# One stage's VectorE and ScalarE order left to the scheduler, its weight loads moved to the GpSimd queue, and the last output piece copied by one engine

## The chip, the cores and the metric

The kernel runs on one core of a Trainium2 chip. The metric is the device time in microseconds. Five engines take instructions, each in the order of its own queue: TensorE (PE in the profile) multiplies, VectorE (DVE) and ScalarE (ACT) work on tiles, GpSimd (POOL) and SyncE (SP) here only issue transfers (DMAs). SBUF holds the tiles, PSUM the sums of products.

## The reference

```python
# attention with decay: B, H, S, D = 4, 8, 768, 64
for t in range(S):
    state = gamma * state + outer(k[:, :, t], v[:, :, t])
    y[:, :, t] = scale * q[:, :, t] @ state
x = y.transpose(0, 2, 1, 3).reshape(3072, 512)
# first layer: w_in 512 x 2048, w_out 2048 x 512
h = x @ w_in
x = (h / (1 + exp(-1.702 * h))) @ w_out
# second layer, weights of the same sizes
h = x @ w_in2
P = a0 + a1*h + a2*h*h + a3*h*h*h
Q = 1 + abs(b0)*abs(h) + abs(b1)*h*h
out = (P / (Q + 1e-6)) @ w_out2
```

The inputs are 64-bit numbers as far as the weights go: a weight unit is read as pairs of 32-bit words.

## The kernel before

The 3072 tokens go in six blocks of 512. The first layer has 16 steps to a block, 96 in all, numbered through. In step j TensorE makes 12 products into a PSUM bank `hp` (`g1`, L1122). ScalarE takes the sigmoid z of it (`act1_a`, L1229), VectorE multiplies z by hp (L1230), and with that the bank is free. ScalarE rounds z to a high part gh (`act1_b`, L1238), VectorE takes the low part gl (L1239). Two steps later TensorE adds 12 products of gh and gl into four banks `o` (`g2`, L1143 to L1145). There are two banks for hp, which the attention's pY takes turns in too. So hp of step j+2, or pY and hp, can begin only when z of an earlier step has left its bank.

Three other things run beside the steps:

- The attention of the later blocks: one unit of 128 tokens (`att_unit`, L954) at four of a block's 16 steps. Its inputs are loaded (L735), scaled and turned by VectorE (`att_turn`), stored (L823) and fetched (L831), all by SP.
- The conversion of the second layer's weights, `conv2`: 32 units, four to a group g. A unit is loaded raw (`raw2`, L629 and L631) into one of four slots of 512 KB (pool `ws`, tag `s`). ScalarE begins (`w_first`, L561, "first" in this text), VectorE does four operations (L567, L569, L572, L583), ScalarE casts the high part (L619), VectorE takes the low part (L620). GpSimd stores it (`put`, L653 and L655). Between units 1 and 2 of a group come four sums (L682). `conv0` says at which step a group starts; a group takes the places x = -1 to 9, one a step.
- At a block's end the four banks `o` are copied (`evac`, L1153 and L1155) into tiles that take slots of the same pool `ws`, and stored by SP (L1156).

`step(i)` writes all this in a fixed order, the conversion at the end of the step. Steps 14 to 77 stand under `tc.manual_schedule(engines={E.PE, E.DVE, E.Activation, E.SP})`: on these four engines the order of the code is kept. On GpSimd, and in the steps from 78 on, a scheduler sets the order at build time: among the instructions that it takes to be ready, it picks the one that stands first in the code. `behind` keeps the raw loads in the code's order. The second layer follows in an order that its own planner writes. Its last output block is copied and stored in four pieces (`evac` inside `layer2`, L271 to L274).

Of the kernel before, what the change touches and what calls it, by code (L numbers as in the profile page):

```python
# [18 lines left out]
P = 128  # L19
# [4 lines left out]
KD = DM // P  # L24
# [37 lines left out]
def layer2(tc, pools, ab, XT, x_tile, XC, WC, WOT, load_wo, held, psum, out):  # L62
    nc = tc.nc
# [3 lines left out]
    NG = KF // 2  # L67
# [34 lines left out]
    for s in range(NSB):  # L102
        for g in range(NG):
            prev = [(s, g - 1, P4)] if g else []
            p = [(s, g, x) for x in (P1, P5, P6, P2, P3, P7)]
# [31 lines left out]
    def start_of(eng, deps):  # L137
        if any(d not in end for d in deps):
            return None
        return max([free[eng]] + [end[d] + (0.35 if d[0] in "PO" else 0.2) for d in deps])  # L140
# [4 lines left out]
    def h_any(half, n, name, dtype=F32):  # L145
        home, tag = SLOT[half, n]
        return home.tile([P, 2, 512], dtype, tag=tag, name=name)
# [114 lines left out]
    def evac(s, half, d):  # L262
        rows = s * 1024 + half * 512 + d * P
        last = (s, half) == (NSB - 1, 1)
        if last:
            t = h_any(0, d, f"os{s}_{half}_{d}")
            cut = 2 if d == 3 else 1
            for y in range(cut):
                m = slice(y * DM // cut, (y + 1) * DM // cut)
                if y or d % 2 and cut == 1:  # L270
                    nc.vector.tensor_copy(out=t[:, 0, m], in_=ACC[d][:, m])  # L271
                else:
                    nc.scalar.copy(out=t[:, 0, m], in_=ACC[d][:, m])
                nc.sync.dma_start(out=out[rows : rows + P, m], in_=t[:, 0, m])  # L274
            return
        if d % 2 == 0:
            EV[0] = h_any(half, 6 * half + d // 2, f"os{s}_{half}_{d}")
        t = EV[0]
        nc.scalar.copy(out=t[:, d % 2], in_=ACC[d])
        if d % 2:  # L280
            nc.sync.dma_start(out=out[rows - P : rows + P, :].rearrange("(x p) m -> p x m", p=P), in_=t)
# [103 lines left out]
    E = mybir.EngineType  # L385
    with tc.manual_schedule(engines={E.PE, E.DVE, E.Activation}):
# [7 lines left out]
        while pe < len(PEQ) or ready["DVE"] or ready["ACT"]:  # L394
            best = None
            if pe < len(PEQ):
# [4 lines left out]
                t = start_of("PE", deps)  # L401
                if t is not None:
                    best = (t, 0, "PE", None)
            for eng in ("DVE", "ACT"):
                c = [(start_of(eng, x[3]), x[2], n) for n, x in enumerate(ready[eng])]
                c = [x for x in c if x[0] is not None]
                if c:
                    t0 = min(x[0] for x in c)
                    _, rank, n = min((x for x in c if x[0] <= t0 + 0.05), key=lambda x: (x[1], x[2]))
# [3 lines left out]
            t, _, eng, n = best  # L413
            name = ("PE",)
            if eng == "PE":
                free["PE"] = t + 1.36
                if it[0] == "P":
                    s, g, p = PROD[it[1]]
# [10 lines left out]
            if name[0] in ("c4", "d3", "d7"):  # L429
                s, g = name[1:]  # L430
# [22 lines left out]
            while waiting and None in slots:  # L453
                m = min(waiting)
# [17 lines left out]
def tile_kernel(ctx: ExitStack, tc: tile.TileContext, q, k, v, w1i, w1o, w2i, w2o, pa, pb, cst, out):  # L472
    nc = tc.nc
# [47 lines left out]
    def unit(layer, u):  # L521
        return (ORD if layer == 1 else ORD2)[u]
# [86 lines left out]
    NG = KF // 2  # L609
# [3 lines left out]
    def behind(dma):  # L613

        tc.keep_in_program_order(dma)
# [6 lines left out]
    def raw2(u):  # L622

        nm, f = unit(2, u)
        src = {"i": w2i, "o": w2o}[nm].bitcast(I32)
        s = ws.tile([P, DM, 2], I32, tag="s", name=f"s2_{u}")
        if nm == "i":
            src = src[:, f * 2 * P : (f + 1) * 2 * P].rearrange("(c p) f -> p c f", p=P)
            behind(nc.sync.dma_start(out=s.rearrange("p (c f) t -> p c (f t)", c=KD), in_=src))  # L629
        else:  # L630
            behind(nc.sync.dma_start(out=s.rearrange("p f t -> p (f t)"), in_=src[f * P : (f + 1) * P, :]))  # L631
        STG[u] = RW[u] = s

    def word2(u):
        w_first(u)
        w_bits(u)
        w_sign(u, False)
# [4 lines left out]
    def parts(key, src, home):  # L642

        n = src.shape[1] // (2 * P)
        t = home.bitcast(F32R).rearrange("p a b -> p (a b)").rearrange("p (x h c) -> p x h c", x=n, h=2)
        split((t[:, :, 0], t[:, :, 1]), src.rearrange("p (x c) -> p x c", c=2 * P))
        OUT2[key] = t

    def put(key):
        t = OUT2.pop(key)  # L650
        g, x = key
        if x == "o":
            nc.gpsimd.dma_start(out=WO[g], in_=t.bitcast(F32))  # L653
        else:
            nc.gpsimd.dma_start(out=WC[g][x].rearrange("x p h k f -> p x (h k f)"), in_=t.rearrange("p x h c -> p x (h c)").bitcast(F32))  # L655

    def whole(f, src, home):
        t = home.bitcast(F32R).rearrange("p a b -> p (a b)").rearrange("p (h c) -> p h c", h=2)
        split((t[:, 0], t[:, 1]), src)
        OUT2[f, "o"] = t  # L660

    def conv2(g, x):

        u = 4 * g
        if x == -1:
            raw2(u)
        elif x == 0:
            raw2(u + 1)
            word2(u)
        elif x == 1:  # L670
            parts((g, 0), STG[u], RW.pop(u))
        elif x == 2:
            put((g, 0))
            word2(u + 1)
        elif x == 3:
            raw2(u + 2)
            a, b = STG.pop(u), STG.pop(u + 1)
            a11, a12, a21, a22 = a[:, : 2 * P], a[:, 2 * P :], b[:, : 2 * P], b[:, 2 * P :]
            t = SUM[g] = ws.tile([P, 4, 2 * P], F32, tag="s", name=f"sum{g}")
            A22S[g] = a22  # L680
            for y, p, q, op in ((0, a21, a22, ALU.add), (1, t[:, 0], a11, ALU.subtract), (2, a11, a21, ALU.subtract), (3, a12, t[:, 1], ALU.subtract)):
                nc.vector.tensor_tensor(out=t[:, y], in0=p, in1=q, op=op)  # L682
            parts((g, 1), t[:, 0:2].rearrange("p x c -> p (x c)"), RW.pop(u + 1))
        elif x == 4:
            put((g, 1))
        elif x == 5:
            raw2(u + 3)
            word2(u + 2)
            t = SUM.pop(g)
            parts((g, 2), t[:, 2:4].rearrange("p x c -> p (x c)"), RW.pop(u + 2))  # L690
            parts((g, 3), A22S.pop(g), t[:, 0:2])
        elif x == 6:
            put((g, 2))
            put((g, 3))
        elif x == 7:
            word2(u + 3)
            e = ws.tile([P, DM, 2], I32, tag="s", name=f"wo{2 * g}s")
            whole(2 * g, STG.pop(u + 2), e)
        elif x == 8:
            put((2 * g, "o"))  # L700
            whole(2 * g + 1, STG.pop(u + 3), RW.pop(u + 3))
        elif x == 9:
            put((2 * g + 1, "o"))
# [520 lines left out]
    def act1_a(j):  # L1224
        n = steps[j][4]
        hp = HP.pop(j)
        z = ch.tile([P, n], F32, tag="z", name=f"z{j}")
        CH[j] = z
        nc.scalar.activation(out=z, in_=hp, func=ACTF.Sigmoid, scale=1.702)  # L1229
        nc.vector.tensor_tensor(out=z, in0=hp, in1=z, op=ALU.mult)  # L1230
# [54 lines left out]
    for u in range(NU):  # L1285
        t = stage_tag(u)
# [9 lines left out]
    E = mybir.EngineType  # L1296
    with tc.manual_schedule(engines={E.SP}):
# [207 lines left out]
        conv0 = [KF + 2 + 9 * g - (0, 0, 0, 0, 1, 2, 3, 4)[g] for g in range(NG)]  # L1505
# [13 lines left out]
        def x_piece(i):  # L1519
            left = 2  # L1520
            while xq and left and (xq[0][0] or i > XS0 + 8):
# [10 lines left out]
                else:  # L1532
                    left -= 1
                    for f in xr[s, kk][n]:
                        if f:
                            f()

        def step(i):
            nonlocal nxt, j
            while nxt < NS and nxt - lead[steps[nxt][0]] <= i:  # L1540
                j = nxt
                nxt += 1
                g1(j)
                act1_a(j)
            if 0 <= i - KF + 2 < WHOLE:
                w_high(1, LATER[i - KF + 2], False)
                w_low(1, LATER[i - KF + 2], False)
            if i == KF:
                tc.keep_in_program_order(nc.scalar.activation(out=ab[:, 6:7], in_=ab[:, 5:6], func=ACTF.Abs))
            late = [f() for f in todo[i][0]]  # L1550
            if j >= FIRST_STEPS + 2 and j in CH:
                act1_b(j)
            for f in late:
                if f:
                    f()
            g2(i)
            layer, bi, fc, t0, n = steps[i]
            if fc == KF - 1 and bi < 5:
                evac(bi)
            late = [f() for f in todo[i][1]]  # L1560

            if i >= XS0:
                x_piece(i)
            if i >= NS - 4:
                load_wo(2 * (i - NS + 4))
                load_wo(2 * (i - NS + 4) + 1)
            if i == XS0 + 4:
                for kk in range(2):
                    t = xp.tile([P, 2, 512], F32, tag=f"xh{kk}_0", name=f"xb{kk}")
                    XB.append(t)  # L1570
                    for c in range(2):
                        nc.sync.dma_start(out=t[:, c], in_=x2[4][2 * c + kk])
            for g in range(NG):
                x = i - conv0[g]
                if x == 9:
                    conv2(g, x)
            for g in range(NG):
                x = i - conv0[g]
                if -1 <= x < 9:
                    conv2(g, x)  # L1580
            for f in late:
                if f:
                    f()

        with tc.manual_schedule(engines={E.PE, E.DVE, E.Activation, E.SP}):
            for i in range(FIRST_STEPS, XS0):
                step(i)
        for i in range(XS0, NS):
            step(i)
# [32 lines left out]
```

## Time and profile before

| | us |
|---|---|
| median of 3 runs (lowest, highest) | 1193.75 (1192.49, 1194.94) |
| the profiled execution | 1192.8 |
| its span | 1191.0 |
| TensorE busy in the span | 1119.5 (94%) |
| VectorE busy | 868.8 (73%) |
| ScalarE busy | 655.2 (55%) |
| GpSimd busy | 31.1 (3%) |

The profile is of one execution. Its time is 1.8 us above its span, which starts with the first instruction and ends with the last transfer. A row of the timeline is: start, duration, engine, line, operation, output and inputs, and in brackets the time that the engine had idled just before, with what ended that idle time. "SPq" and "POOLq" are the queues' DMA issues. Lines are those of the kernel before; in the kernel after, lines behind L684 are higher by 1 or 2.

### The profile page before, as it was taken

To read this page: it belongs to the slowest core of one execution; us is meant where nothing else is said; L and a number is where in the kernel's file an instruction comes from. 1 tells how busy PE (TensorE), PEld (TensorE's weight loads), DVE (VectorE), ACT (ScalarE), POOL (GpSimd) and SP (SyncE) were. 2 spreads that over 40 slices of the span, in tenths; PEclk is the share of its full clock that TensorE was granted. 3 is DMA by queue.
4 is the path that set the end of the run, shared out by engine and by line. 5 is a ranking of instruction groups with operands and counts; after the bars stand their busy time and mean duration, and the time that the engine had idled before them with its cause. 6 is when DMAs were issued, how large, how long until landed. Compare 5 with 4: busy or idle time off the path is not lost.

```text
span 1191.0 us, 18828 instructions
## 1 busy us (share of the span) xinstructions
PE 1119.5 (94%) x7217; PEld 911.8 (77%) x7217; DVE 868.8 (73%) x1192; ACT 655.2 (55%) x987; POOL 31.1 (3%) x52
## 2 busy tenths in 40 slices
PE   8999999698996879797999999999999999999998
PEld 6688878577775757586888888888888888888887
DVE  6999646375564445455577679999889899789895
ACT  5998322132232322222354569978778786787782
POOL 0000000000000000000000000000000000000000
PEclk9999999889998989899999999999999999999999
DMA  9944557565564554565278798583345561354100
GB/s 238 326 129 115 113 127 164 151 159 153 139 157 133 141 147 120 156 168 160 95 261 297 230 325 286 195 297 153 91 129 153 184 247 46 122 157 122 43 36 36
DMA packets 230394, 193.54 MB, mean 163 GB/s; under 512 B 153888, under 2 KB 178976, under 8 KB 230304
## 3 DMA queue, kind: packets, MB, share of 16 engines
q1 hardware_dynamic: 223904, 169.27, 49.4%
q0 software_dynamic: 6400, 23.07, 5.3%
q8 instruction: 57, 0.93, 0.3%
q14 instruction: 33, 0.27, 0.1%
HBM read 134.48 MB, written 57.67 MB: 161 GB/s over the span
## 4 chain that ended last, share of the span: by engine, by line
PE 66%; SPq 11%; DMA 9%; DVE 5%; issue 3%; ACT 2%; DVEq 0%; ACTq 0%
PE o L256 22%; PE hp L1122 13%; PE a L157 11%; SPq L735 7%; PE c L157 5%; DMA s<-in_moe_w_out_dram 4%; PE o L1143 3%; PE o L1144 3%; PE o L1145 3%; PE b L157 3%; DMA s<-in_moe_w_in_dram 2%; DMA xs<-x 2%; SPq L831 2%; SPq L823 1%; PE pY L954 1%
## 5 line engine op out<-in xcount | busy, mean ns | idle before, releaser
L1122 PE MATMUL hp<-xh,wi 128*128 128x512 f32 x768 | 266.7, 410 | 44.5 <-DVE z L1230 42.8
L1122 PEld LDWEIGHTS hp<-xh,wi 128*128 128x128 f32 x768 | 150.8, 196 | 81.8 <-DVE z L1230 45.9
L1122 PE MATMUL hp<-xl,wi 128*128 128x512 f32 x384 | 154.8, 404 | 0.0
L157 PE MATMUL a<-x,wi 128*128 128x512 f32 x576 | 145.3, 390 | 0.0
L1143 PE MATMUL o<-gh,wo 128*128 128x512 f32 x368 | 144.5, 393 | 0.0
L1144 PE MATMUL o<-gl,wo 128*128 128x512 f32 x368 | 143.6, 390 | 0.0
L1145 PE MATMUL o<-gh,wo 128*128 128x512 f32 x368 | 143.4, 390 | 0.0
L567 DVE TENSOR_SCALAR u<-u 128x512 f32<-128x512 f32 x64 | 27.0, 422 | 139.7 <-ACT u L561 139.7
L561 ACT ACTIVATE u<-s 128x512 f32<-128x512 f32 x64 | 43.1, 675 | 151.7 <-DMA s<-in_moe_w_in_dram 86.7
L157 PEld LDWEIGHTS a<-x,wi 128*128 128x128 f32 x576 | 108.0, 188 | 22.9 <-ACT b L180 0.4
L1238 ACT CAST gh<-z 128x512 fp32r<-128x512 f32 x80 | 49.6, 620 | 99.6 <-DVE z L1230 99.6
L1229 ACT ACTIVATE z<-hp 128x512 f32<-128x512 f32 x80 | 47.6, 595 | 86.3 <-PE hp L1122 80.1
L1230 DVE TENSOR_TENSOR z<-hp,z 128x512 f32<-128x512 f32 x80 | 54.9, 686 | 44.8 <-ACT z L1229 36.7
L1122 PEld LDWEIGHTS hp<-xl,wi 128*128 128x128 f32 x384 | 75.9, 198 | 15.2 <-issue 0.3
L320 DVE SCALAR_TENSOR_TENSOR z<-z,ab,w 128x1024 f32<-128x1024 f32 x48 | 61.6, 1283 | 28.4 <-ACT w L318 28.4
L1143 PEld LDWEIGHTS o<-gh,wo 128*128 128x128 f32 x368 | 69.7, 189 | 15.1 <-DVE wo L605 0.4
L1239 DVE TENSOR_TENSOR gl<-z,gh 128x512 fp32r<-128x512 f32 x80 | 54.7, 684 | 36.1 <-ACT gh L1238 35.0
L1144 PEld LDWEIGHTS o<-gl,wo 128*128 128x128 f32 x368 | 69.4, 189 | 14.6 <-DVE gl L1239 0.2
L1145 PEld LDWEIGHTS o<-gh,wo 128*128 128x128 f32 x368 | 69.2, 188 | 14.5
L157 PE MATMUL c<-x,wi 128*128 128x512 f32 x288 | 73.1, 389 | 0.0
L334 ACT ACTIVATE gh<-h 128x1024 fp32r<-128x1024 f32 x48 | 50.9, 1060 | 34.1 <-PE o L256 33.5
L338 DVE SCALAR_TENSOR_TENSOR gl<-h,gh 128x1024 fp32r<-128x1024 f32 x48 | 58.8, 1224 | 5.4 <-ACT gh L334 5.4
(246 smaller groups left out, 2203.5 us busy)
## 6 DMA issues: line engine op xcount, KB each, us to landing
wi<-wc SPq DMA_DIRECT2D x168, 256.0 KB, 2.9
s<-in_moe_w_in_dram SPq DMA_DIRECT2D x32, 512.0 KB, 5.6
s<-in_moe_w_out_dram SPq DMA_DIRECT2D x32, 512.0 KB, 5.2
x<-xc SPq DMA_DIRECT2D x28, 512.0 KB, 8.5
wc<-s POOLq DMA_DIRECT2D x24, 512.0 KB, 3.9
xc<-xo SPq DMA_DIRECT2D x36, 256.0 KB, 2.7
x<-os SPq DMA_DIRECT2D x20, 256.0 KB, 2.5
xs<-x SPq DMA_DIRECT2D x20, 256.0 KB, 4.3
```

Source lines behind the costliest of these rows:

```text
L157: nc.tensor.matmul(bank, wt[:, a, k], XT[s, x, k][:, b], start=begin and y == 0, stop=y == 5, skip_group_check=True)
L256: nc.tensor.matmul(ACC[d], a[:, x, r], w[:, b], start=g == 0 and x == 0 and y == 0, stop=g == NG - 1 and x == 1 and y == 2)
L320: dve("q", [("ab", m)], lambda: stt(out=v["z"], in0=v["z"], scalar=ab[:, 6:7], in1=v["w"], op0=ALU.mult, op1=ALU.add))
L334: nc.scalar.activation(out=GT[m][0], in_=h, func=ACTF.Copy, scale=-1.0)
L338: nc.vector.scalar_tensor_tensor(out=gl, in0=h, scalar=-1.0, in1=gh.bitcast(F32), op0=ALU.mult, op1=ALU.subtract)
L735: nc.sync.dma_start(out=t[HALF[n], NP * x : NP * x + NP, :], in_=heads[x])
L1122: nc.tensor.matmul(hp, w[:, kk, :], t[kk // 2][:, kk % 2, :], start=(x == 0), stop=(x == len(terms) - 1))
L1143: nc.tensor.matmul(o, wl[:, r], gh, start=a, stop=False)
L1144: nc.tensor.matmul(o, wh[:, r], gl, start=False, stop=False)
L1145: nc.tensor.matmul(o, wh[:, r], gh, start=False, stop=z)
L1230: nc.vector.tensor_tensor(out=z, in0=hp, in1=z, op=ALU.mult)
L1239: nc.vector.tensor_tensor(out=gl, in0=z, in1=gh.bitcast(F32), op=ALU.subtract)
```

## The change

The raw loads go from SP's queue to GpSimd's. Their place in the code stays at the end of the step (`conv2_load`), while the rest of `conv2` is called one step later, ahead of the step's own second half (`convert`). VectorE and ScalarE are taken out of the engines whose order is kept in steps 14 to 77. In the last output piece the second half is copied by ScalarE instead of VectorE and stored from ScalarE's queue.

```diff
-                if y or d % 2 and cut == 1:
+                if d % 2 and cut == 1:
                     nc.vector.tensor_copy(out=t[:, 0, m], in_=ACC[d][:, m])
                 else:
                     nc.scalar.copy(out=t[:, 0, m], in_=ACC[d][:, m])
-                nc.sync.dma_start(out=out[rows : rows + P, m], in_=t[:, 0, m])
+                (nc.scalar if y else nc.sync).dma_start(out=out[rows : rows + P, m], in_=t[:, 0, m])
...
-            behind(nc.sync.dma_start(out=s.rearrange("p (c f) t -> p c (f t)", c=KD), in_=src))
+            behind(nc.gpsimd.dma_start(out=s.rearrange("p (c f) t -> p c (f t)", c=KD), in_=src))
...
-            behind(nc.sync.dma_start(out=s.rearrange("p f t -> p (f t)"), in_=src[f * P : (f + 1) * P, :]))
+            behind(nc.gpsimd.dma_start(out=s.rearrange("p f t -> p (f t)"), in_=src[f * P : (f + 1) * P, :]))
...
+    def conv2_load(g, x):
+        n = {-1: 0, 0: 1, 3: 2, 5: 3}.get(x)
+        if n is not None:
+            raw2(4 * g + n)
...
+        def convert(i):
+            for g in sorted(range(NG), key=lambda g: i - conv0[g] != 9):
+                if 0 <= i - conv0[g] <= 9:
+                    conv2(g, i - conv0[g])
...
                 g1(j)
                 act1_a(j)
+            convert(i - 1)
...
             for g in range(NG):
-                x = i - conv0[g]
-                if x == 9:
-                    conv2(g, x)
-            for g in range(NG):
-                x = i - conv0[g]
-                if -1 <= x < 9:
-                    conv2(g, x)
+                conv2_load(g, i - conv0[g])
...
-        with tc.manual_schedule(engines={E.PE, E.DVE, E.Activation, E.SP}):
+        with tc.manual_schedule(engines={E.PE, E.SP}):
```

The order on TensorE is the same in both kernels, and SP's is the same without the raw loads. In the rows below z54 is z of step 54, u15 and s2_15 belong to weight unit 15, sum3 to group 3, and the last number of a name only tells tiles apart.

ScalarE from the sigmoid of step 54, before:

```order
L1229 ACTIVATE z54_4397<-hp54_4384 128x512
L1238 CAST gh54_4416<-z54_4397 128x512
L561 ACTIVATE u15_4520<-s2_15_4338 128x512
L619 CAST wo6s_4526<-u14_4340 128x512
L960 CAST xh4_0_4172<-pY_17_4432 128x2x128
L960 CAST xh4_1_4173<-pY_17_4432 128x2x128
L1229 ACTIVATE z55_4554<-hp55_4541 128x512
```

and in the change:

```order
L1230 ACTIVATE z54_4395<-hp54_4382 128x512
L1239 CAST gh54_4416<-z54_4395 128x512
L619 CAST s2_18_4786<-sum4_4814 128x2x256
L561 ACTIVATE u19_5080<-s2_19_4870 128x512
L619 CAST wo8s_5086<-u18_4888 128x512
L561 ACTIVATE u20_5126<-s2_20_5052 128x512
L619 CAST s2_19_4870<-u19_5080 128x512
L961 CAST xh4_0_4172<-pY_17_4432 128x2x128
L961 CAST xh4_1_4173<-pY_17_4432 128x2x128
L1230 ACTIVATE z55_4545<-hp55_4532 128x512
```

Between the same two sigmoids ScalarE now begins two units, 19 and 20, where it began unit 15.

VectorE from z of step 52 to z of step 53, before:

```order
L1230 TENSOR_TENSOR z52_4319<-hp52_4306,z52_4319 128x512
L1239 TENSOR_TENSOR gl52_4323<-z52_4319,gh52_4322 128x512
L567 TENSOR_SCALAR u14_4340<-u14_4340 128x512
L569 TENSOR_SCALAR s2_14_4256<-s2_14_4256 128x512
L572 SCALAR_TENSOR_TENSOR u14_4340<-u14_4340,s2_14_4256 128x512
L583 SCALAR_TENSOR_TENSOR u14_4340<-s2_14_4256,u14_4340 128x512
L620 TENSOR_TENSOR s2_14_4256<-sum3_4258,s2_14_4256 128x2x256
L620 TENSOR_TENSOR sum3_4258<-u13_4114,sum3_4258 128x256
L1230 TENSOR_TENSOR z53_4363<-hp53_4350,z53_4363 128x512
```

and in the change, from z of step 51 to z of step 52:

```order
L1231 TENSOR_TENSOR z51_4279<-hp51_4266,z51_4279 128x512
L567 TENSOR_SCALAR u15_4548<-u15_4548 128x512
L620 TENSOR_TENSOR wo6s_4554<-u14_4356,wo6s_4554 128x512
L1240 TENSOR_TENSOR gl51_4290<-z51_4279,gh51_4289 128x512
L572 SCALAR_TENSOR_TENSOR u15_4548<-u15_4548,s2_15_4338 128x512
L567 TENSOR_SCALAR u16_4594<-u16_4594 128x512
L583 SCALAR_TENSOR_TENSOR u15_4548<-s2_15_4338,u15_4548 128x512
L569 TENSOR_SCALAR s2_16_4520<-s2_16_4520 128x512
L572 SCALAR_TENSOR_TENSOR u16_4594<-u16_4594,s2_16_4520 128x512
L620 TENSOR_TENSOR s2_15_4338<-u15_4548,s2_15_4338 128x512
L583 SCALAR_TENSOR_TENSOR u16_4594<-s2_16_4520,u16_4594 128x512
L1231 TENSOR_TENSOR z52_4318<-hp52_4305,z52_4318 128x512
```

The work of two units is now mixed between z and gl of one step, and unit 16 comes at step 51; before it comes at step 55.

GpSimd's queue around the units 14 to 18, before:

```order
L655 DMA wc3_2_117<-s2_14_4256 128x2x512
L655 DMA wc3_3_118<-sum3_4258 128x512
L653 DMA wo6_141<-wo6s_4526 128x1024
L653 DMA wo7_142<-s2_15_4338 128x1024
L655 DMA wc4_0_119<-s2_16_4529 128x2x512
```

and in the change:

```order
L631 DMA s2_15_4338<-in_moe2_w_out_dram 128x1024
L655 DMA wc3_3_118<-sum3_4282 128x512
L629 DMA s2_16_4520<-in_moe2_w_in_dram 128x4x256
L655 DMA wc3_2_117<-s2_14_4256 128x2x512
L653 DMA wo6_141<-wo6s_4554 128x1024
L629 DMA s2_17_4573<-in_moe2_w_in_dram 128x4x256
L653 DMA wo7_142<-s2_15_4338 128x1024
L655 DMA wc4_0_119<-s2_16_4520 128x2x512
L631 DMA s2_18_4786<-in_moe2_w_out_dram 128x1024
```

The loads of units 15 to 18 now stand among the stores; unit 16's load stands ahead of unit 14's store, unit 18's behind that of unit 16.

## Rows read from the trace of the kernel before

**Rows 1.** Table by stretches: length, then busy time (instructions) by engine, clock, DMA.

```profile
core 0: us, PE busy (x) PEld busy (x) DVE busy (x) ACT busy (x) POOL busy (x), PEclk, DMA share, GB/s
...
149.46:606.75 457.29, 393.99 (x3369) 323.54 (x3368) 245.48 (x447) 124.88 (x234) 27.06 (x42) 0.93 0.56 147
606.75:697.19 90.44, 90.17 (x397) 74.09 (x396) 63.85 (x107) 43.47 (x75) 3.86 (x6) 1.00 0.81 284
```

**Rows 2.** Timeline, ScalarE's sigmoids of steps 74, 75 and 76.

```profile
569.59 0.60 ACT L1229 ACTIVATE z<-hp 128x512 f32<-128x512 f32 x1 [0.88 <-PE hp L1122]
577.31 0.60 ACT L1229 ACTIVATE z<-hp 128x512 f32<-128x512 f32 x1 [2.30 <-PE hp L1122]
582.75 0.60 ACT L1229 ACTIVATE z<-hp 128x512 f32<-128x512 f32 x1 [3.46 <-PE hp L1122]
```

**Rows 3.** TensorE's waits, 149.46 to 606.75 us: total, times, longest.

```profile
PE hp L1122 <- DVE z L1230: 42.5, 9, 9.6
PE pY L954 <- DVE z L1230: 17.2, 6, 4.1
PE pK L954 <- DMA rawv<-in_v_dram: 3.1, 1, 3.1
```

**Rows 4.** Chain of waits (start, length), and the table by stretches, around 240 us.

```profile
240.95 4.69 PE hp L1122 x12
...
248.38 2.72 PE hp L1122 x12
```

```profile
240.00:245.00 5.00, 4.05 (x10) 3.22 (x11) 4.93 (x10) 1.68 (x4) 0.00 (x0) 0.54 0.22 52
```

**Rows 5.** Timeline of ScalarE, 418 to 442 us.

```profile
423.13 0.62 ACT L619 CAST s<-u 128x512 fp32r<-128x512 f32 x1
437.04 0.66 ACT L561 ACTIVATE u<-s 128x512 f32<-128x512 f32 x1 [13.30 <-DMA s<-in_moe_w_in_dram]
437.61 0.58 ACT L1229 ACTIVATE z<-hp 128x512 f32<-128x512 f32 x1
```

**Rows 6.** Timeline of TensorE, 440 us.

```profile
440.60 0.79 PE L1122 MATMUL hp<-xh,wi 128*128 128x512 f32 x1 [8.15 <-DVE z L1230]
```

**Rows 7.** Timeline of SP's issues, 418 to 434 us.

```profile
421.55 5.29 SPq L735 DMA_DIRECT2D rawq<-in_q_dram  x4
...
432.27 1.09 SPq L629 DMA_DIRECT2D s<-in_moe_w_in_dram  x2
```

**Rows 8.** ScalarE's waits, 149.46 to 606.75 us.

```profile
ACT u L561 <- DMA s<-in_moe_w_in_dram: 86.7, 7, 15.5
...
ACT u L561 <- DMA s<-in_moe_w_out_dram: 56.5, 8, 10.4
```

**Rows 9.** DMA issues: queue, count, KB each, median us to landing.

```profile
wc<-s POOLq DMA_DIRECT2D x21, 512.0 KB, 3.9
s<-in_moe_w_in_dram SPq DMA_DIRECT2D x16, 512.0 KB, 4.9
...
x<-os SPq DMA_DIRECT2D x12, 256.0 KB, 2.6
...
wo<-wo14s POOLq DMA_DIRECT2D x1, 512.0 KB, 7.0
```

**Rows 10.** One line's instructions, POOL's stores: ns min, median, max.

```profile
L655 POOL DMA_DIRECT2D wc<-s x24: 707/732/837, 173.1 to 632.3; - x24
```

**Rows 11.** Timeline of ScalarE, VectorE and SP at the end.

```profile
1187.17 0.37 ACT L273 COPY os<-o 128x256 f32<-128x256 f32 x1 [0.77 <-PE o L256]
1187.58 0.42 DVE L271 COPY os<-o 128x256 f32<-128x256 f32 x1 [2.43 <-ACT os L273]
1187.57 0.81 SPq L274 DMA_DIRECT2D out_dram<-os  x2
```

**Rows 12.** SP's waits, 149.46 to 606.75 us.

```profile
SPq L629 <- DMA wc<-s: 21.7, 1, 21.7
SPq L631 <- DMA wc<-s: 12.0, 1, 12.0
```

More of the change, by code (lines that the diff above doesn't have):

```diff
@@ L660, in whole @@
         OUT2[f, "o"] = t
+    def conv2_load(g, x):
+        n = {-1: 0, 0: 1, 3: 2, 5: 3}.get(x)
+        if n is not None:
+            raw2(4 * g + n)
     def conv2(g, x):
         u = 4 * g
[L665 to L668, printed above, removed]
+        if x == 0:
             word2(u)
@@ L675, in conv2 @@
         elif x == 3:
-            raw2(u + 2)
             a, b = STG.pop(u), STG.pop(u + 1)
@@ L686, in conv2 @@
         elif x == 5:
-            raw2(u + 3)
             word2(u + 2)
```

## The prediction

> **What bounds the kernel now.** I read three views: the table by stretches, the waits of TensorE, and ScalarE's rows around one wait. The stretch from the sigmoid of step 19 (149.46 us) to that of step 80 (606.75 us) lasts 457.29 us, and TensorE is busy for 393.99 us of it at a mean granted clock of 0.93; in the 90.44 us behind it TensorE is busy for 90.17 at 1.00 [rows 1]. So what can be won lies in this stretch.
>
> How long would it take undisturbed? Three sigmoids of a quiet place stand at 569.59, 577.31 and 582.75 [rows 2]: a step without an attention unit takes 5.44 us, one with a unit 7.72, so a unit costs 2.28. The stretch has 61 steps and 16 units: 61 x 5.44 + 16 x 2.28 = 368.3 us. It loses 457.3 - 368.3 = 89.0 us. TensorE's waits account for 42.5 + 17.2 + 3.1 = 62.8 us, in 16 waits, 15 of them for the multiplication z (L1230) that empties an hp bank [rows 3]. The other 26 us, 1.6 us a wait, are work at the lower clock: behind one of these waits twelve matmuls took 4.69 us, where two steps of work later they took 2.72, and the granted clock of the 5 us around them was 0.54, so mostly the lower level, 1.2 GHz [rows 4].
>
> Why is z late? At 423.13 us ScalarE begins a cast of 0.62 us and then stands for 13.30 us before `first` (L561) of unit 16, whose raw weights come by DMA; the sigmoid of step 56 is queued behind it and goes at 437.61 [rows 5]. z of step 56 follows and TensorE has idled 8.15 us [rows 6]. The weights were late because SP issues them in its own order: from 421.55 it was busy with twelve attention loads and got to the weights at 432.27 [rows 7]. In sum ScalarE stood 86.7 + 56.5 = 143.2 us in 15 such waits [rows 8].
>
> **The change, part by part.** TensorE's order is the same row by row, and SP's too but for the 32 weight loads that leave it. Four things are new.
>
> (1) The weight loads stand on POOL, between the stores of finished pieces. SP is freed of 32 issues and of their slot waits. On POOL a load can wait only behind stores of earlier units.
>
> (2) VectorE and ScalarE take the conversion early, whenever the scheduler thought them idle, and so in bursts. By the order, the 32 units lie behind z of steps 18 to 24 (units 0 to 6), 33 to 38 (7 to 13), 49 to 55 (14 to 21), 65 to 71 (22 to 29) and 81 to 85 (30 and 31). In the 7 to 9 steps between two bursts no sigmoid has a load before it, and I take the loss there as nothing: VectorE and ScalarE have then only a step's two operations each, and the attention's, beside TensorE's 5.44 us.
>
> (3) Inside a burst VectorE is the engine to watch. Its mean instruction in the stretch is 245.48 / 447 = 0.549 us [rows 1]. From the order, the steps of the bursts hold 77, 72, 84, 84 and 41 instructions of VectorE: 42.3, 39.5, 46.1, 46.1 and 22.5 us. TensorE needs for the same steps (7, 6, 7, 7 and 5 steps, with 2, 2, 2, 2 and 0 units) 42.6, 37.2, 42.6, 42.6 and 27.2 us. VectorE has too much by 0, 2.3, 3.5, 3.5 and 0 us.
>
> To this come its own waits. In the third burst the sum of group 3 takes a slot of the block's output tile, so it waits for the store of that tile (2.6 us to landing [rows 9]), about 2 us that nothing fills. Units 15, 16 and 17 are loaded behind the store of unit 13 and land 4.9 us after issue [rows 9]; followed by hand, each is there up to 0.8 us after VectorE wants it. I take 4 us a burst. What VectorE may lag before TensorE stops: around an attention unit the hp after it needs z of the hp before it, 2.72 + 2.28 = 5.0 us later, less sigmoid and z (0.60 + 0.7): 3.5 to 3.7. I take 3.5. TensorE then stands 0.5, 2.8, 4.0 and 4.0 us in the first four bursts, 11.3 together, none in the fifth. The clock takes 1.6 us a wait; with some six waits, 10 us. For loads that land later than the middle value I add 1 us a burst, 4. New loss: 11 + 10 + 4 = 25 us, so 64 us are won.
>
> The price of a load on POOL is not in the trace. Stores of the same 512 KB from POOL land after 3.9 us, at worst 7.0; loads from SP after 4.9 [rows 9]. POOL itself takes 0.71 to 0.84 us for a store [rows 10]. So a load lands between 3.9 and 7.0; I take 4.9, the row of the same transfer, and keep 3.9 and 7.0 for the range.
>
> The Trainium skill (SBUF — State Buffer, section "SBUF: two separate sides") has a rule against this: while VectorE runs an fp32 operation in a two-port mode, GpSimd cannot write the descriptors of its DMAs. By it each of six loads in four bursts could start one VectorE operation later (0.55 us at the mean), 13 us in all, and the time would be 1143. By the rows alone it adds 3 at most: POOL's stores, issued between the same VectorE operations, took at most 0.84 us against a least 0.71 [rows 10], a spread of 0.13 us.
>
> (4) The last output piece. Now VectorE starts its half at 1187.58, after ScalarE's half has ended, and SP issues the two stores from 1187.57 [rows 11]. With both halves on ScalarE the second ends 0.05 us sooner (0.37 against 0.42) and its store need not wait for SP's queue. A first store on ScalarE's queue is not in the trace: bounds -0.4 (SP's issue gone) and +0.8 (both issues together on SP last 0.81). I take -0.1, next to the copy's row.
>
> Sum, against the profiled execution: 1192.8 - 64 - 0.1 = 1128.7 us. The median of the runs is 0.95 us above that execution: 1129.7, which I round to 1130.
>
> **Rivals.**
> A. The loads come late. Six loads of a burst are within about a microsecond of being waited for. If each lands at the far end, 7.0 instead of 4.9, four bursts x six x 2.1 us = 50 us come back: about 1180. For it: in a burst stores and loads of the same slots share one queue in order, and the traffic is denser. Against: nothing in the trace at POOL reaches 7.0 but one store.
>
> B. The bursts cost nothing. If VectorE's lag never reaches TensorE, the loss is only the clock after a few short waits, about 7 us: 1112. For it: 3.5 us of slack is the tightest place, 6.9 the usual one (three groups of twelve matmuls less 1.3). Against: 46.1 us of work for 42.6.
>
> C. Slower: the units run one after the other. POOL's queue holds a store that waits for VectorE ahead of a load that the next unit needs. Where this closes the ring for every unit, a unit takes landing 4.9, `first` 0.66, four VectorE operations 2.2, cast 0.62, low part 0.55 and the store's landing 3.9: 12.8 us [rows 5, 9]. The four bursts have 30 units, 385 us, where TensorE needs 165: a loss of 220 against the 89 of now, 1324 us. It decides from (165 + 89) / 30 = 8.5 us a unit. Against: by POOL's order unit 16's load stands before unit 14's store, so two or three units are under way at once.
>
> D. No change: slots and not queues hold up the loads. Two of SP's waits in the stretch, of 21.7 and 12.0 us, were for the slot that a weight load writes to, until a store had landed [rows 12]. If the ring of four slots sets the pace, moving the issue to POOL moves the waits along, and the time stays at 1192 to 1196. Against it: in the wait of [rows 5] SP was busy with twelve attention issues for 10.7 us, up to the weights [rows 7]. The Trainium skill (DMA: Bandwidth & Descriptors, section "Issuing engines are not separate DMA queues") is on D's side: issuing from another engine saves only sequencer time, usually little. Here the trace shows that this time is not little.
>
> **How the numbers follow.** The forecast gets 0.57, with a range of its own from 1114 to 1148; A 0.19, between 1148 and 1188; B 0.10; C 0.09; D 0.05. The range for 8 in 10 goes from 1108, below B, to 1176, through most of A. About 0.2% (2.4 us) is what a measurement of this kernel can tell from no change. Faster: 0.57 + 0.19 + 0.10 = 0.86. Same: D's 0.05. Slower: C's 0.09.
>
> **What would show it.** In the stretch of steps 19 to 80: about 393 us between the two sigmoids instead of 457; ScalarE's waits for the two weight tensors far below 143 us; no wait of TensorE over 5 us; the waits that are left at the bursts, with VectorE busy over 0.9 there and under 0.5 between them; the rest of the kernel within 1 us of before. If TensorE stands at the bursts with VectorE idle and ScalarE before L561, it is A, or C where every unit shows it. If it stands between the bursts, something I have not seen is late. The forecast is wrong if VectorE's rows in a burst sum to much more than 46 us, or if a load from POOL takes over 7 us to land.

## The result, and the profile after

| | before | after |
|---|---|---|
| median (lowest, highest), 4 runs each | 1194.35 us (1192.49, 1196.3) | 1157.39 us (1155.52, 1158.46) |
| ratio, 95% interval | | 0.969 (0.967 to 0.971) |
| span of the profiled execution | 1191.0 us | 1156.1 us |
| sigmoid of step 19 to that of step 80 | 457.29 us | 422.11 us |
| of it above 368.3 us | 89.0 us | 53.8 us |
| TensorE's waits there | 62.8 us | 37.6 us |

The change is faster by 37 us, where 64 were forecast. All of it lies in the stretch that the prediction looked at: 35.2 us there, 34.9 in the whole span of the profiled executions. So the stretch, with its bursts, is the place to look for the missing 27 us.

The table by stretches of the kernel after: the whole stretch, the third burst (from the sigmoid of step 50 to that of step 57), the gap behind it, and the fourth burst (66 to 73).

```profile
core 0: us, PE busy (x) PEld busy (x) DVE busy (x) ACT busy (x) POOL busy (x), PEclk, DMA share, GB/s
149.40:571.51 422.11, 384.51 (x3369) 315.14 (x3368) 249.55 (x456) 129.13 (x237) 47.87 (x73) 0.96 0.62 163
370.06:425.21 55.15, 47.49 (x415) 38.65 (x414) 40.88 (x80) 20.89 (x39) 12.51 (x19) 0.94 0.84 238
425.21:466.51 41.30, 41.30 (x404) 34.23 (x403) 19.83 (x33) 9.81 (x19) 0.59 (x1) 1.00 0.47 96
477.45:531.30 53.85, 47.13 (x436) 38.47 (x435) 40.99 (x80) 20.61 (x39) 12.42 (x19) 0.97 0.87 246
```

The first row answers to [rows 1]. In the gap TensorE is busy without a break at the full clock, 2.4 GHz. Each of these bursts has 42.6 us of work for TensorE, by the prediction's count of seven steps and two units, and they last 55 and 54 us. VectorE is busy for 0.74 and 0.76 of it, not over 0.9: it is not full, it waits too.

TensorE's waits in the stretch after, with the columns of [rows 3]:

```profile
PE hp L1123 <- DVE xl L963: 16.0, 5, 6.4
PE hp L1123 <- DVE z L1231: 12.5, 5, 5.0
PE pK L955 <- DMA rawv<-in_v_dram: 5.3, 3, 3.1
PE pY L955 <- DVE z L1231: 2.0, 2, 1.1
PE pY L955 <- issue: 1.8, 1, 1.8
```

What was 59.7 us behind z is 14.5 now. A new line stands at the top: xl, VectorE's low part of the attention's result (L963), cost 0.4 us of waiting before. Where the longest of these waits, 6.42 us, comes from is seen in four timelines, GpSimd's, VectorE's, ScalarE's and TensorE's, between 177 and 186 us:

```profile
177.31 0.77 POOL L629 DMA_DIRECT2D s<-in_moe_w_in_dram  x1 [4.80 <-issue]
```

```profile
182.95 0.43 DVE L569 TENSOR_SCALAR s<-s 128x512 int32<-128x512 uint32 x1 [3.88 <-DMA s<-in_moe_w_in_dram]
...
184.26 0.76 DVE L963 TENSOR_TENSOR xl<-pY,xh 128x256 fp32r<-128x256 f32 x2
```

```profile
183.01 0.69 ACT L561 ACTIVATE u<-s 128x512 f32<-128x512 f32 x1 [5.34 <-DMA s<-in_moe_w_in_dram]
183.59 0.64 ACT L961 CAST xh<-pY 128x256 fp32r<-128x256 f32 x2
```

```profile
185.16 0.77 PE L1123 MATMUL hp<-xh,wi 128*128 128x512 f32 x1 [6.42 <-DVE xl L963]
```

The load of unit 5 leaves GpSimd at 177.31 and lands 5.7 us later. ScalarE has stood for 5.34 us before its first operation, VectorE for 3.88 before L569, which needs nothing but the load. The attention's xh and xl are queued behind these two, and TensorE starts when xl is there. This is the wait of [rows 5] again, shorter, and on two engines. What GpSimd waited for in the 4.80 us ahead of this load the profile does not show ("issue").

ScalarE's waits for the two weight tensors, which answer to [rows 8]:

```profile
ACT u L561 <- DMA s<-in_moe_w_in_dram: 50.8, 15, 6.5
ACT u L561 <- DMA s<-in_moe_w_out_dram: 18.7, 7, 4.3
```

They went from 143.2 us to 69.5, and from 15 waits to 22. Why the loads are late is to be seen in GpSimd's own waits over the stretch, here the first two of its rows for loads (25.5 of 49.5 us; the other rows name other causes or none), and in its timeline in the third burst:

```profile
POOL s L629 <- DMA wc<-s: 16.3, 7, 3.5
POOL s L631 <- DMA wc<-s: 9.2, 3, 3.2
```

```profile
387.89 0.77 POOL L629 DMA_DIRECT2D s<-in_moe_w_in_dram  x1 [3.50 <-DMA wc<-s]
...
391.58 0.71 POOL L655 DMA_DIRECT2D wc<-s  x1 [2.12 <-DVE s L620]
...
400.58 0.71 POOL L655 DMA_DIRECT2D wc<-s  x1 [6.17 <-DVE s L620]
401.29 0.58 POOL L631 DMA_DIRECT2D s<-in_moe_w_out_dram  x1
...
404.86 0.76 POOL L629 DMA_DIRECT2D s<-in_moe_w_in_dram  x1 [2.43 <-DMA wc<-s]
...
413.46 0.75 POOL L629 DMA_DIRECT2D s<-in_moe_w_in_dram  x1 [1.79 <-DMA wc<-s]
```

```profile
393.61 0.66 ACT L561 ACTIVATE u<-s 128x512 f32<-128x512 f32 x1 [3.25 <-DMA s<-in_moe_w_in_dram]
...
411.10 0.68 ACT L561 ACTIVATE u<-s 128x512 f32<-128x512 f32 x1 [1.72 <-DMA s<-in_moe_w_in_dram]
...
419.45 0.67 ACT L561 ACTIVATE u<-s 128x512 f32<-128x512 f32 x1 [6.12 <-DMA s<-in_moe_w_in_dram]
```

The loads at 387.89, 404.86 and 413.46 go out when the store that frees their slot has landed, and the unit begins 5.7, 6.2 and 6.0 us after its load went out. That is one of two causes. The load at 401.29 leaves right behind a store that had waited 6.17 us for VectorE; the store that freed its own slot had left at 391.58 and landed 5.0 us later, at 396.6. Of the 30 loads in the stretch ten follow the landing of a store, and twelve stand in GpSimd's queue behind a store that waits for VectorE.

Of units 15 to 21, the first begins at 381.27 and the last at 419.45: 38.2 us for six, 6.4 us a unit. Seven or eight units in the 42.6 us that TensorE needs would be 5.3 to 6.1.

### The profile page after: what moved, and what is told of

It reads as the page before. It is cut to its first block, busy times and chain, and to the rows that moved or that the text cites. A ratio compares the mean times of both kernels' runs of the same rounds, so it can differ in the third digit from the quotient of the medians.

```text
span 1156.1 us, 18811 instructions
## 1 busy us (share of the span) xinstructions
PE 1109.2 (96%) x7216; PEld 903.3 (78%) x7217; DVE 867.2 (75%) x1191; ACT 658.0 (57%) x988; POOL 52.7 (5%) x84
## 4 chain that ended last, share of the span: by engine, by line
PE 52%; issue 14%; DMA 6%; DVE 2%; POOL 1%; ACT 1%; SPq 0%; POOLq 0%; ACTq 0%; DVEq 0%
PE o L256 23%; PE a L157 11%; PE c L157 6%; PE hp L1123 4%; PE b L157 3%; DMA s<-in_moe_w_in_dram 3%; PE o L1145 2%; PE o L1144 2%; PE o L1146 2%; DMA xs<-x 1%; DMA s<-in_moe_w_out_dram 1%; DMA xc<-xo 1%; DMA wc<-sum 1%; POOL wc L655 1%; ACT u L561 0%
## 5 line engine op out<-in xcount | busy, mean ns | idle before, releaser
L561 ACT ACTIVATE u<-s 128x512 f32<-128x512 f32 x64 | 43.3, 678 | 77.6 <-DMA s<-in_moe_w_in_dram 51.6
L1146 PEld LDWEIGHTS o<-gh,wo 128*128 128x128 f32 x368 | 69.3, 188 | 14.5
L1145 PEld LDWEIGHTS o<-gl,wo 128*128 128x128 f32 x368 | 69.4, 189 | 14.4
L157 PEld LDWEIGHTS c<-x,wi 128*128 128x128 f32 x288 | 54.1, 188 | 11.2
```

The source lines that it names most:

```text
L157: nc.tensor.matmul(bank, wt[:, a, k], XT[s, x, k][:, b], start=begin and y == 0, stop=y == 5, skip_group_check=True)
L1145: nc.tensor.matmul(o, wh[:, r], gl, start=False, stop=False)
L1146: nc.tensor.matmul(o, wh[:, r], gh, start=False, stop=z)
```

## The experiments

Theory S says that the bursts outrun the supply: four slots, each taken from the load's issue until the store's landing, gave a unit every 6.4 us, where TensorE's pace asks for one every 5.3 to 6.1. Rival V is the prediction's own step, a VectorE that is too full. Rival L is a GpSimd queue that loads slowly in itself, rival Q the attention's work, which the scheduler also moved on VectorE. The kernel before was timed anew beside each group of runs (1190 us in all of them), so kernels of different groups are compared by their ratio to it. The changed kernel's is 0.969.

**Less work for VectorE.** In the changed kernel:

```diff
     def word2(u):
         w_first(u)
-        w_bits(u)
+        nc.vector.tensor_scalar(out=U[u], in0=U[u], scalar1=2.0, scalar2=MAXF, op0=ALU.max, op1=ALU.min)
         w_sign(u, False)
```

> The changed kernel with two of the four VectorE operations of a weight unit left out (the scaling of the low word, L569, and the OR, L572), so the low bits of the second layer's weights are not put in; loads, stores and ScalarE's operations stay, and the units lie in the same bursts (steps 18 to 23, 34 to 38, 50 to 54, 66 to 70). Theory S, supply: inside a burst each unit waits for its raw load, which waits on GpSimd's queue for the store that frees one of the four slots; VectorE stands idle there. Then 32 x 1.1 us less of VectorE work buys little: 1150 to 1158 us, and ScalarE still waits 55 us or more at L561 for loads. Theory V, VectorE too full in the bursts (the step of the prediction): 7.7 us less work for seven units takes it below TensorE's 42.6 us in every burst, so most of the 54 us of loss goes: 1110 to 1130 us.

Measured: 1163.74 us, ratio 0.978 (0.975 to 0.981), so not faster than the change but a little slower. The stretch, and under it TensorE's longest waits there:

```profile
149.96:571.83 421.87, 382.26 (x3369) 312.90 (x3368) 223.59 (x396) 129.75 (x237) 47.45 (x73) 0.96 0.63 163
```

```profile
PE hp L1123 <- DVE xl L963: 24.1, 4, 8.9
PE hp L1123 <- DVE z L1231: 11.5, 5, 3.2
```

VectorE has 26 us less to do (223.59 for 249.55), and the stretch is 0.2 us shorter; ScalarE waits 69.4 us for loads, as after. V falls. S had 1150 to 1158: the profile fits, the time is above. Units 15 to 21 begin 6.0 us apart here instead of 6.4, and yet TensorE waits 8 us longer for xl, so the pace alone does not set its waits.

**Both orders as written, loads on GpSimd.** In the changed kernel:

```diff
-        with tc.manual_schedule(engines={E.PE, E.SP}):
+        with tc.manual_schedule(engines={E.PE, E.DVE, E.Activation, E.SP}):
```

> The changed kernel with VectorE and ScalarE back in the order of the code for steps 14 to 77; loads stay on GpSimd, the conversion stays one step behind its load. Units then come one at a time, two or three steps apart. Theory S: a load has a step and a half (8 us or more) from issue to its first use and lands in about 5.7 us, a slot is free long before it is wanted, so the waits at L561 nearly vanish: 1105 to 1122 us. Theory V gives the same, as there are no bursts. Rival L, GpSimd's queue is slow for loads in itself: ScalarE's waits stay above 50 us and the time above 1140 us.

Measured: 1117.40 us, ratio 0.940 (0.937 to 0.943). The stretch is 11.7 us above the quiet time:

```profile
149.97:529.92 379.95, 371.92 (x3374) 307.57 (x3373) 247.01 (x448) 125.85 (x236) 44.83 (x70) 0.99 0.69 176
```

ScalarE has no wait at L561 for a load. L falls with it: loads of the two tensors land after 5.0 and 6.2 us at the median, near the 5.7 and 5.9 after the change, but nobody stands for them. Only the order on these two engines was put back, and 35 us of 1157 go with it, more than the 27 that were missing.

**The queue alone.** In the kernel before, `nc.sync` becomes `nc.gpsimd` at L629 and L631.

> The kernel before with nothing changed but the queue of the raw loads: GpSimd instead of SP. Theory S: the lateness of before came from SP's queue alone, and here the units stay spread, so most of the 89 us of loss goes; with a step less of distance than in the run with both orders manual, a few loads are a microsecond or two late: 1110 to 1130 us. Rival L as above: above 1150 us. Rival D of the prediction (slots set the pace): 1188 to 1196 us.

Measured: 1114.77 us, ratio 0.937 (0.934 to 0.940). The stretch, TensorE's waits in it, the only row, and ScalarE's at L561, the only row for a load:

```profile
151.61:529.04 377.43, 371.99 (x3377) 308.10 (x3376) 249.14 (x450) 128.57 (x238) 45.55 (x71) 0.99 0.70 180
```

```profile
PE pK L954 <- DMA rawv<-in_v_dram: 5.4, 3, 4.3
```

```profile
ACT u L561 <- DMA s<-in_moe_w_in_dram: 0.5, 1, 0.5
```

So the queue alone is worth 75 us: the stretch takes 377.4 us, 80 less, and the kernel gives 3.5 back ahead of it and behind it. The rest of the change takes back half of it. The step of distance that `convert` adds is worth nothing here. Rival D of the prediction falls: the ring of four slots was not what set the pace before. GpSimd waits 16.6 us for `wc<-s` ahead of a load here too (25.5 after the change), and ScalarE stands 0.5 us: such a wait costs only where the unit is wanted at once.

**The order alone.** In the changed kernel the loads go back to SP.

> The changed kernel with the raw loads back on SP: the scheduler's order on VectorE and ScalarE, the conversion one step behind, the last piece as in the change. Theory S: SP still comes late to a load when attention issues stand before it, so ScalarE still waits over 100 us at L561 and the time is 1165 to 1200 us. If the order alone made the gain, it would be at 1157 us or below.

Measured: 1137.83 us, ratio 0.956 (0.952 to 0.960). The expectation was wrong. ScalarE waits 36.1 us for loads, not over 100:

```profile
ACT u L561 <- DMA s<-in_moe_w_in_dram: 25.5, 12, 5.3
...
ACT u L561 <- DMA s<-in_moe_w_out_dram: 10.6, 5, 4.4
```

Here the loads keep their places on SP, in the written order, and by the order of this kernel the scheduler puts the units at steps 22 to 87 with at most two behind one step, not in four bursts. So the scheduler's order, together with the step of distance, is worth 52 us where the loads are on SP; no run has the step of distance alone there, so what each is worth is not shown. Where the loads are on GpSimd the order costs 35 us (0.969 against 0.940): the two parts of the change are no sum. What the scheduler makes of a load depends on the queue that it stands on.

**ScalarE alone as written.** The diff of the second run without `E.DVE`.

> The changed kernel with ScalarE alone put back in the order of the code for steps 14 to 77; VectorE stays with the scheduler, whose order of the attention's VectorE work (rawq, rawk, xl) is again its own. ScalarE's first operation of a unit then comes at steps 21, 23, 26, 28 and so on, not in bursts, and VectorE's follow it. Theory S (bursts outrun the loads of the four slots): no late loads at L561, 1110 to 1122 us. Rival Q (it is the attention's work, moved by the scheduler on VectorE, that holds up TensorE): most of the loss of 54 us stays, above 1140 us.

Measured: 1137.14 us, ratio 0.956 (0.953 to 0.959): between the two. VectorE's waits in the stretch, in their order of size:

```profile
DVE s L569 <- DMA s<-in_moe_w_out_dram: 41.5, 14, 5.7
DVE z L1231 <- ACT z L1230: 34.4, 25, 3.4
DVE rawq L817 <- DMA rawq<-in_q_dram: 34.3, 10, 4.4
DVE s L569 <- DMA s<-in_moe_w_in_dram: 25.6, 7, 4.7
```

L569 needs no result of ScalarE, so the scheduler still puts it early, and VectorE stands 67 us for raw loads. The three waits of TensorE for xl (6.7 us) each come behind such a wait:

```profile
175.17 0.43 DVE L569 TENSOR_SCALAR s<-s 128x512 int32<-128x512 uint32 x1 [5.73 <-DMA s<-in_moe_w_out_dram]
175.51 0.42 DVE L974 TENSOR_TENSOR st<-pK,st 128x256 f32<-128x256 f32 x1
175.84 0.68 DVE L977 TENSOR_TENSOR sm<-pS,cs 128x512 f32<-128x512 f32 x1
176.44 0.75 DVE L963 TENSOR_TENSOR xl<-pY,xh 128x256 fp32r<-128x256 f32 x2
```

```profile
177.33 0.47 PE L1123 MATMUL hp<-xh,wi 128*128 128x512 f32 x1 [1.63 <-DVE xl L963]
```

Q does not fit these places: it is a load again, not the attention's own inputs, that xl stands behind. S as I had put it (1110 to 1122) misses too, since it looked only at ScalarE's queue: one engine that comes early to a load is enough, without a burst on the other. Whether the 34.3 us before `rawq` cost TensorE something in other places stays open.

**Five slots.** To find 4 KB a partition, the pool of gh and gl loses a buffer, in the control and in the test; the test then has

```diff
-    ws = l1.enter_context(tc.tile_pool(name="ws", bufs=4))
+    ws = l1.enter_context(tc.tile_pool(name="ws", bufs=5))
```

> Control for the next run: the changed kernel with the pool of gh and gl at two instead of three buffers, four slots for the raw weights as before. gl of a step may then come only when the products of two steps before are done. Both theories: within 10 us of the changed kernel, 1150 to 1167 us.

> As the control, with five slots of 512 KB instead of four (the space comes from the pool of gh and gl). The scheduler still places the units in bursts, somewhat tighter (three units behind one step in places). Theory S: a slot is free sooner, so loads are issued earlier and ScalarE waits less for them: 10 to 30 us below the control, and GpSimd's waits for a store before a load shrink. Rival: if four slots were enough and only the landing time of a load counts, no more than 5 us below the control.

Measured: control 1173.10 us, ratio 0.988 (0.984 to 0.991), outside what I expected for it; five slots 1149.25 us, ratio 0.965 (0.960 to 0.969). GpSimd's waits for `wc<-s`, the most frequent store, before a load, first of the control, then with five slots (none of L631 in the second):

```profile
POOL s L629 <- DMA wc<-s: 15.0, 7, 3.7
...
POOL s L631 <- DMA wc<-s: 10.0, 3, 3.8
```

```profile
POOL s L629 <- DMA wc<-s: 7.5, 2, 4.0
```

ScalarE's waits for loads, in the same order:

```profile
ACT u L561 <- DMA s<-in_moe_w_in_dram: 47.4, 14, 6.9
ACT u L561 <- DMA s<-in_moe_w_out_dram: 22.5, 8, 4.6
```

```profile
ACT u L561 <- DMA s<-in_moe_w_in_dram: 29.1, 9, 4.5
ACT u L561 <- DMA s<-in_moe_w_out_dram: 14.3, 7, 3.1
```

A fifth slot takes 25.0 us of these waits to 7.5, ScalarE's waits for loads from 69.9 us to 43.4, and 24 us off the time, with the units in bursts as before. S holds, for a part of the loss: 43.4 us of waits for loads are left, and with five slots too loads stand in GpSimd's queue behind stores that wait for VectorE (unit 18's at 382.31 us, behind a wait of 4.33). No run changes that queue's order alone, so its share is not shown. The scheduler's order shifts a little with the slot, so the 24 us are of both together.

**VectorE alone as written.** The diff of the second run without `E.Activation`.

> The changed kernel with VectorE alone put back in the order of the code; ScalarE stays with the scheduler. ScalarE's first operations lie a step or two earlier than in the code's order (steps 18, 19, 24, 26, 28, 29, 33 and so on), but not in bursts. Theory S: 1112 to 1130 us, a few loads are wanted early. Rival Q: about the same, since VectorE has the code's order.

Measured: 1123.06 us, ratio 0.945 (0.943 to 0.948), as both expected; ScalarE waits 6.4 us for loads in four waits.

**The last piece alone, and with the queue.**

> The kernel before with the last output piece alone as in the change: both halves copied by ScalarE, the second stored from its queue. From the last matmul to the end of the span 0.05 to 0.2 us less than before (3.8 us there), which the timing cannot tell from none: a ratio of 0.998 to 1.002.

> The kernel before with the raw loads on GpSimd's queue and the last piece as in the change; the orders of VectorE and ScalarE stay as written. The run with the queue alone took 1114.8 us; the last piece adds or takes nothing that shows: 1112 to 1117 us, below both kernels of the case.

Measured: the last piece alone 1188.25 us, ratio 0.998 (0.997 to 1.000), which cannot be told from none. From the start of TensorE's last row to the end of the span it is 4.48 us before, 4.36 in this run and 4.39 after: 0.1 us. Queue and last piece together: 1114.92 us, ratio 0.936 (0.934 to 0.938), the same as the queue alone. By the ratios the queue, with or without the last piece, is 3.3 to 3.4% below the change.

## Why the prediction was right and where it was wrong

- The measured 1157 us lies in the range for 8 in 10, but outside the forecast's own range of 1114 to 1148 and inside rival A's. That the wide range held is in part luck: it took in most of A, and the loads were late by another cause than the one A names.
- What bounds the kernel now: right. Late loads on SP held up the sigmoid. With the queue alone TensorE's waits behind z are gone, and the loss of 89 us falls to 9. The waits went, and the lower clock with them: 0.93 in [rows 1], 0.99 without bursts.
- SP freed of 32 issues, step (1): right, and larger than the whole forecast, 75 us. The Trainium skill (DMA: Bandwidth & Descriptors, section "Issuing engines are not separate DMA queues") expects little of another issuing engine. Here a load no longer stands behind attention issues; the 75 us decide.
- No loss between the bursts, step (2): right but for two waits for `rawv` behind the first burst (3.1 and 1.9 us, at 235 and 237 us), which before, with 3.1 us in [rows 3], have their like.
- Inside a burst "VectorE is the engine to watch", step (3): wrong, and the step that failed. With 26 us of VectorE's work gone, the stretch stayed as long. The term under it, "each is there up to 0.8 us after VectorE wants it", was made with a load that leaves when GpSimd's queue comes to it. It leaves when its slot's store has landed, or when a store ahead of it in the queue has got its result from VectorE, which is the cause that rival C names. C's price was 12.8 us for a turn of a slot, and I used it only to ask when the change would be slower (8.5 us a unit), not what a pace of 6.4 does. The price was too low as well: from the load's issue to the store's landing units 15 to 20 held their slots for 16.5 to 21.1 us, 18.8 at the mean, which at 6.4 us a unit is about three units under way (a group's sums and one of its output tiles take slots of the pool as well). That 12.8 us over two units gives 6.4 too is chance.
- The size: 11.3 us of waits for TensorE became 37.6, and where 14 us stood for the clock and late loads, 16.2 us are left beside the waits. So 25 became 53.8.
- The signs: TensorE's longest wait was to stay within 5 us and is 6.42, VectorE was to be busy over 0.9 in the bursts and is at 0.74 and 0.76. What the prediction's list gives for this picture, TensorE standing at the bursts with VectorE idle and ScalarE before L561, is A or C, not the forecast. The rest of the kernel moved by 0.3 us, as said.
- The slack of 3.5 us was taken for VectorE's lag behind z. The attention's xh and xl, which stand behind a unit on both engines, have their own, and 16.0 us of the 37.6 are theirs.
- A load from GpSimd lands after 5.7 and 5.9 us, between my 4.9 and 7.0. Rival A put the lateness in the landing; it lay in when the load was issued.
- The Trainium skill's rule on GpSimd's descriptors beside VectorE (SBUF — State Buffer, section "SBUF: two separate sides") is not seen here: in the stretch after too GpSimd took 0.71 to 0.79 us for a store `wc<-s` of 512 KB. Which operations of VectorE run in a two-port mode no run shows.
- The last piece, step (4): 0.1 us, as forecast.

What stays open: how the loss in the bursts divides between the slots and the order of GpSimd's queue, and why the scheduler draws the units together when their loads are on GpSimd. The runs show that it does and what it costs, not how it decides.

## What to carry to other kernels

When a transfer that others wait for stands in a queue behind work that it has nothing to do with, move that transfer alone first, and time it, before anything else is given a new order. When work is drawn together into a burst, divide the time that one buffer is held (load's landing, work, store's landing, as measured) by the buffers that these units really have: that is the pace of the burst, however idle the engines are. Look also at what stands ahead of each load in its queue: a store that waits there for an engine holds the load back though its buffer is free. And look at every engine that reads the buffer: an instruction put early on an in-order queue waits there with all that stands behind it.

## What the runs showed of the hardware

Landing times hardly moved with the order: loads of the two tensors landed after 5.7 and 5.9 us (medians) with the change and after 5.2 and 5.8 with the queue alone, though the DMA engines were busy for 0.84 of the third burst and 0.70 of the other kernel's stretch. I had expected denser traffic to show there. Giving up one of three buffers of gh and gl cost 22 us (0.988 against 0.969), though TensorE's waits for gh and gl in the control add up to 1.6 us; its waits for xl and z are 4.5 us longer. Some 10 us lie ahead of the stretch: the sigmoid of step 19 comes at 159.87 us in the control and at 149.40 after the change, and the attention ahead of it takes tiles of the same pool. The rest I cannot place.
